# First stage of a fused linear-attention and gated-MLP kernel: work in turns that every engine keeps, with another order of norms, folds, products and sums

## The chip, the cores and the metric

One core of a Trainium2 chip runs the kernel. The metric is the device time of one execution in microseconds (us); several executions are timed, and the median is given.

## What is computed

The input `x` has 2048 rows (tokens) of 1024 numbers, all float32. Cut to what matters:

```
xn = layernorm(x)
q, k, v = split(xn @ wqkv)                # 32 heads of 32
pq, pk = q @ w_phi, k @ w_phi             # per head, 32x32
phi = concat(softmax(p), softmax(-p))     # for q and for k
o = phi_q (phi_k^T v) / (phi_q . sum(phi_k))
s = o @ wo
g = silu((sigmoid(xn @ w_gate) * (xn @ w_up)) @ w_down)
out = x + s * g
```

## The kernel before, in words

The matrix products are done by a scheme that halves both matrices in both directions and needs seven block products, with sums of blocks ahead of and behind them, in place of eight. The seven block products have names: B11, B21, T2, T3, T4, T1, B22, in this order for the projections (`order`, line 366). Each is carried out in split float32: an operand is kept as a rounded high part and a rest (`split`, line 173: a cast on ScalarE, line 175, and a difference on VectorE, line 176), and each product is three matmuls (`mm3`, line 178: lines 180, 181, 182).

Tokens go in two halves (c = 0 and 1) of 1024, in tiles of 128. For each half the stages are: projections to v, k and q (`ops`, line 372), then the gate and up products, and at the end down products, attention and output. One block product of a projection ("a group" below) is four units u, one for each tile of 128 tokens of a block, of four k steps of three matmuls 128x512: 48 matmuls. B21 is added in the same bank (PSUM) as B11, so B11's unit is copied out first (`proj_out`, line 456: lines 468 and 471 on ScalarE, 465 on VectorE).

The first stage makes what these groups need:

- `x_load` (201) loads a tile of x; `norm_steps` (205) makes statistics on VectorE (212, 213, 215), a square root on ScalarE (216), six small operations on VectorE (218 to 224) and the normalizing itself on ScalarE (227).
- `transpose` (241) does eight 128x128 transposes on TensorE (247) into two of the four banks of the ring `tps` (197). For tiles 0 to 3 the two blocks are split into operands of B11 and B21 (`operand`, 233) and also copied out (250).
- `x_sums` (252) subtracts blocks on GpSimd, in pieces of 128x256 (`Pieces`, line 79), for T1, T3, T2 and T4, and splits T2's and T3's operands at once; `x_rest` (839) splits those of B22, T1 and T4.
- v's weights are loaded in four blocks of 1 MB (`v_load`, 306), used straight by B11 and B21, summed (`v_sums`, 310: half on VectorE, line 315, half on GpSimd) for the others and stored in DRAM. `prep` (410) splits the next 128x1024 of weights into a ring of eight slots.
- The weights of k and q are folded with w_phi (`fold`, 348): for each of four k a set of four loads from `wqkT`, four times four small matmuls against a block-diagonal matrix `bd` (357), a copy (361 for k, 359 for q) and four sums on GpSimd and seven stores (`w_sums`, 283). They take their banks from the same ring `tps`.

The order before: tile 0 is traced under a high priority, the rest hangs in a deque `side`, of which `step()` runs one item after each unit of the projection (line 946). The program is scheduled ahead of time by a model that fills an engine's idle time with what is ready by its reckoning and comes earliest in the trace, so the order on each engine need not be that of the trace. `tc.issue_after(i)` puts the instructions of a block that run on the engine of i behind i in that engine's queue, without a wait for its end. SyncE (SP) issues all loads and stores in one queue.

Of the kernel before, what the change touches and what calls it, by code (L numbers as in the profile page):

```python
# [94 lines left out]
def hedgehog_glu_kernel(  # L95
# [90 lines left out]


    side = deque()

# [8 lines left out]

    last_norm = []
# [5 lines left out]
    def norm_steps(tiles, xs):  # L205
        n = len(tiles)
# [22 lines left out]
    def norm(tiles, xs):  # L229
        for _ in norm_steps(tiles, xs):  # L230
# [10 lines left out]
    def transpose(t, xt, dst):  # L241

        th, u = t // 4, t % 4
        for q in range(2):
            tp = tps.next()
            for k in range(4):
                nc.tensor.transpose(tp[:, k * P:(k + 1) * P], xt[:, (4 * q + k) * P:(4 * q + k + 1) * P], ident)
            if th == 0:
                operand(0, (B11, B21)[q], u, tp)
            nc.scalar.copy(dst[q], tp)  # L250

    def x_sums(c, u, first, second):
        (b11, b21), (b12, b22) = first, second
        t2 = b22 if c else b12
        for i, o, a, b in ((T1, b11, b12, b11), (T3, b12, b22, b12), (T2, t2, b22, b11), (T4, b21, b21, t2)):
            pool.sub(o, a, b)
            if c or i in (T2, T3):
                operand(c, i, u, o)

# [46 lines left out]
    def v_load(i):  # L306
        r, f, kh = ((39, 0, 0), (41, 0, 1), (45, 1, 0), (36, 1, 1))[i]
        nc.sync.dma_start(row4(r), v_block(f, kh))

    def v_sums():  # L310
        vec, pl = nc.vector.tensor_tensor, pool.tensor_tensor
        for f, o, a, b, op in ((vec, 3, 2, 3, "add"), (vec, 2, 0, 2, "subtract"),
                               (pl, 0, 3, 0, "subtract"), (pl, 1, 1, 0, "subtract")):
            for h in range(2):
                f(whole(VA[o] + h), whole(VA[a] + h), whole(VA[b] + h), op=getattr(ALU, op))
        for i in (T2, T3, T1, B22):
            nc.sync.dma_start(wf_d[V, i], row4(v_first[i]))

# [27 lines left out]
    o_r = Ring((36, 37, 38))  # L346

    def fold(which, k):

        bs = halves(*fblock[which].next())  # L350
        for b, (f, h) in zip(bs, ((0, 0), (0, 1), (1, 0), (1, 1))):
            r = fraw.next()
            nc.sync.dma_start(r, wqkT[which, f, k + 4 * h].rearrange("p g n -> p (g n)"))
            ps = tps.next()
            for g in range(4):
                gs = slice(g * P, (g + 1) * P)
                nc.tensor.matmul(ps[:, gs], r[:, gs], bd[:, 4 * f + g], start=True, stop=True)
            if which == Q:
                nc.scalar.copy(b.rearrange("p (a g d) -> p g a d", a=2, d=DH), ps.rearrange("p (g a d) -> p g a d", a=2, d=DH))
            else:  # L360
                nc.scalar.copy(b, ps)
        w_sums(which, k, *bs)

# [251 lines left out]
    def x_task(t):  # L615
# [18 lines left out]
        if th:  # L634
            x_sums(1, u, halves(53), halves(54))

# [176 lines left out]


    XS = (24, 25, 26, 27, 52, 53, 24, 25)
    first = [halves(i) for i in (50, 51, 54, 38)]
    b12s, b22s = Ring(halves(10)), halves(8, 9)
    xts = [x_load(0, XS[0])]
    v_load(0)
    xts += [x_load(t, XS[t]) for t in range(1, 4)]  # L820
    v_load(1)
    xts += [x_load(t, XS[t]) for t in range(4, 6)]

    def x_tiles(*tiles):
        norm(tiles, [xts[t] for t in tiles])
        for t in tiles:
            if t < 4:
                transpose(t, xts[t], first[t])
            else:
# [3 lines left out]
            if t < 2:  # L833
                xts.append(x_load(t + 6, XS[t + 6]))
            if t == 1:
                v_load(2)
                v_load(3)

    def x_rest():
        for i, name, src in ((B22, "x1", b22s), (T1, "x2", [b[0] for b in first]), (T4, "x6", [b[1] for b in first])):  # L840
            block(name, XO[i], 4, F32R)
            for u in range(4):
                operand(0, i, u, src[u])
        fraw.items = halves(43, 54)

    with tc.high_priority():
        x_tiles(0)
    with tc.issue_after(last_norm[0]):
        while prep():
            pass  # L850
    one = whole(44)[:, :P]
    nc.gpsimd.memset(one, 1.0)
    nc.scalar.copy(ones, one)
    phraw = whole(47)[:, :KT * DH].rearrange("p (g f) -> p g f", f=DH)
    nc.sync.dma_start(phraw, w_phi.rearrange("(g p) f -> p g f", p=P))
    nc.gpsimd.memset(bd, 0.0)
    for j in range(4):
        nc.gpsimd.tensor_copy(bd[j * DH:(j + 1) * DH, :, j * DH:(j + 1) * DH], phraw[j * DH:(j + 1) * DH])

    def todo(f, *a):  # L860
        side.append(lambda: f(*a))
# [12 lines left out]
    pmm = Ring(banks[:4])  # L874
    gmm = Ring(banks[:4])
    pbank, gbank = {}, {}
    ur = Ring(halves(50, 51))
# [57 lines left out]
    for n, (kind, c, what, i) in enumerate(ops):  # L935
        ws = ready[n]
        if kind == "proj":
            for u in range(4):
                if i in opening:
                    pbank[u] = pmm.next()  # L940
                xo = run(XO[i], 4)
                us = slice(u * P, (u + 1) * P)
                for k in range(4):
                    mm3(pbank[u], (xo[:, k, 0, us], xo[:, k, 1, us]), pair(ws[k]),
                        i in opening and k == 0, k == 3, skip_group_check=True)
                step()
# [281 lines left out]
```

## Time and profile before

| what | us |
|---|---|
| three runs | 2400.01, 2396.53, 2404.08 |
| median | 2400.01 |
| the profiled execution | 2394.26 |
| its span in the trace | 2392.5 |
| TensorE busy in the span | 2345.4 |

The profile is of one execution. TensorE is called PE, its weight loads PEld, VectorE DVE, ScalarE ACT, GpSimd POOL. Times in views are counted from the start of the span. The granted clock is given as a share of full speed. A busy matmul includes its tail in the pipeline, so neighbours overlap. In a view, `<-` behind a group names what it reads, and "[idle before <-releaser]" is how long the engine stood still before it and what ended that.

### The profile page before, as it was taken

The page shows a single profiled execution, that of the slowest core. Times are in us where ns is not written, and L with a number is a line of the kernel's source. Part 1 is how long each engine was busy: PE and PEld are TensorE (multiplying, and loading weights), DVE is VectorE, ACT ScalarE, POOL GpSimd, SP SyncE. Part 2 cuts the span into 40 slices and gives each one's busy share as a digit, 9 for nine tenths or more (in the row PEclk, how much of TensorE's full clock was granted, in tenths as well). Part 3 has the DMA queues.
Part 4 walks back from the last instruction along what each step waited for, and adds up shares of the span by engine and source line. Part 5 has one row for each costly group of instructions (what it writes and reads, how often), then busy time and mean ns, then how long its engine had stood idle before and what let it go on. Part 6 is the DMA issues. An engine that isn't in the chain of part 4 may idle for free.

```text
span 2392.5 us, 32528 instructions
## 1 busy us (share of the span) xinstructions
PE 2345.4 (98%) x10728; PEld 1946.9 (81%) x10728; DVE 1645.7 (69%) x2341; ACT 996.3 (42%) x1482; POOL 1206.9 (50%) x1394
## 2 busy tenths in 40 slices
PE   6999999999999999999999999999999999999998
PEld 5888888888888878887888888888888888888887
DVE  7434788777777666466767778765666786567775
ACT  6432344445454444223434343443434333345442
POOL 5630166757767532305775424244544455533766
PEclk9999999999999999999999999999999999999999
DMA  7884566788888889858998676669777877878664
GB/s 283 261 276 168 169 232 221 259 293 306 298 299 302 278 300 359 297 196 299 346 328 326 228 234 220 229 223 353 244 243 250 274 238 252 283 245 301 207 194 159
DMA packets 266426, 626.23 MB, mean 262 GB/s; under 512 B 37904, under 2 KB 66576, under 8 KB 261648
## 3 DMA queue, kind: packets, MB, share of 16 engines
q1 hardware_dynamic: 266256, 624.15, 76.3%
q8 instruction: 84, 1.38, 0.2%
q14 instruction: 86, 0.70, 0.1%
HBM read 374.47 MB, written 249.56 MB: 261 GB/s over the span
## 4 chain that ended last, share of the span: by engine, by line
PE 59%; POOL 6%; DMA 4%; issue 4%; DVE 2%; ACT 1%; SPq 0%; POOLq 0%; DVEq 0%; ACTq 0%
PE bank L180 19%; PE bank L181 19%; PE bank L182 19%; POOL fc L79 4%; POOL fb L79 1%; PE bank L558 1%; DMA fa<-w_down 1%; DMA fc<-xo_d 1%; POOL x L79 1%; DVE x L176 0%; DMA out<-fc 0%; ACT x L175 0%; DVE w L176 0%; DMA xo_d<-fc 0%; DMA fc<-f_d 0%
## 5 line engine op out<-in xcount | busy, mean ns | idle before, releaser
L181 PE MATMUL bank<-x,w 128*128 128x512 f32 x2352 | 916.3, 390 | 0.0
L180 PE MATMUL bank<-x,w 128*128 128x512 f32 x2352 | 907.0, 390 | 7.9 <-DMA w<-ws_d 4.7
L182 PE MATMUL bank<-x,w 128*128 128x512 f32 x2352 | 905.1, 389 | 0.0
L79 POOL TENSOR_TENSOR fc<-fc 128x256 f32<-128x256 f32 x496 | 420.3, 880 | 455.0 <-DMA fc<-e_d 112.3
L176 DVE TENSOR_TENSOR w<-fa,w 128x512 fp32r<-128x512 f32 (+1 forms) x444 | 406.9, 920 | 196.7 <-ACT w L175 192.6
L175 ACT CAST w<-fa 128x512 fp32r<-128x512 f32 (+1 forms) x444 | 306.8, 698 | 531.2 <-PE bank L181 318.2
L180 PEld LDWEIGHTS bank<-x,w 128*128 128x128 f32 x2352 | 442.1, 188 | 101.9 <-issue 5.1
L182 PEld LDWEIGHTS bank<-x,w 128*128 128x128 f32 x2352 | 442.1, 188 | 91.7
L181 PEld LDWEIGHTS bank<-x,w 128*128 128x128 f32 x2352 | 442.2, 188 | 90.2
L180 PE MATMUL bank<-w,x 128*128 128x512 f32 x708 | 279.2, 395 | 10.5 <-ACT fc L468 4.0
L182 PE MATMUL bank<-w,x 128*128 128x512 f32 x708 | 278.0, 393 | 3.3 <-DVE x L176 3.3
L181 PE MATMUL bank<-w,x 128*128 128x512 f32 x708 | 277.4, 392 | 0.0
L79 POOL TENSOR_TENSOR fb<-fa 128x256 f32<-128x256 f32 x112 | 100.8, 922 | 248.8 <-PE bank L182 129.6
L79 POOL TENSOR_TENSOR fb<-fb,fc 128x256 f32<-128x256 f32 x132 | 121.7, 944 | 140.1 <-DVE fc L1011 138.6
L180 PEld LDWEIGHTS bank<-w,x 128*128 128x128 f32 x708 | 133.9, 189 | 41.8 <-ACT x L175 5.5
L182 PEld LDWEIGHTS bank<-w,x 128*128 128x128 f32 x708 | 133.7, 189 | 32.9 <-DVE x L176 5.6
L181 PEld LDWEIGHTS bank<-w,x 128*128 128x128 f32 x708 | 133.8, 189 | 26.6
L79 POOL TENSOR_TENSOR fc<-fc,sa 128x256 f32<-128x256 f32 x128 | 98.5, 801 | 95.2 <-issue 86.0
L175 ACT CAST p<-fc 128x512 fp32r<-128x512 f32 x100 | 75.4, 758 | 143.8 <-DVE fc L531 61.2
L176 DVE TENSOR_TENSOR x<-fa,x 128x512 fp32r<-128x512 f32 x112 | 92.4, 825 | 49.7 <-ACT x L175 49.4
L176 DVE TENSOR_TENSOR p<-fc,p 128x512 fp32r<-128x512 f32 x100 | 96.4, 970 | 39.0 <-ACT p L175 38.9
L175 ACT CAST w<-fb 128x512 fp32r<-128x512 f32 (+1 forms) x114 | 71.0, 624 | 113.3 <-PE bank L181 85.8
(205 smaller groups left out, 2915.7 us busy)
## 6 DMA issues: line engine op xcount, KB each, us to landing
ws_d<-w SPq DMA_DIRECT2D x112, 512.0 KB, 4.3
w<-ws_d SPq DMA_DIRECT2D x112, 512.0 KB, 5.2
fa<-w_gu SPq DMA_DIRECT2D x84, 512.0 KB, 4.7
fa<-h_d SPq DMA_DIRECT2D x84, 512.0 KB, 5.2
fa<-wf_d SPq DMA_DIRECT2D x32, 1024.0 KB, 6.5
h_d<-fc SPq DMA_DIRECT2D x120, 256.0 KB, 5.2
fa<-w_down SPq DMA_DIRECT2D x80, 256.0 KB, 5.1
h_d<-fb SPq DMA_DIRECT2D x76, 256.0 KB, 4.8
```

Of the source, the lines that this page charges most:

```text
L79: self.engine.tensor_tensor(o[:, s], a[:, s], b[:, s], op=op)
L175: nc.scalar.copy(o[0], src)
L176: return nc.vector.tensor_sub(o[1], src, o[0].bitcast(F32))
L180: nc.tensor.matmul(o, a[0], b[0], start=first, stop=False, **kw)
L181: nc.tensor.matmul(o, a[0], b[1], start=False, stop=False, **kw)
L182: nc.tensor.matmul(o, a[1], b[0], start=False, stop=last, **kw)
L558: nc.tensor.matmul(kvb[g // 2][:, g % 2 * 256:g % 2 * 256 + 256], v[:, g].rearrange("p a f -> p (a f)"), ph[:, g].rearrange("p a f -> p (a ...
```

## The change

A context manager `turn()` is new. Each turn puts every instruction that it traces behind the last instruction, on the same engine, of all turns before. The first stage, with all of the first two groups (B11 and B21 of v, tokens' half 0), is a list of such turns, and the groups' loop skips these two. Within the list:

- w_phi comes in another layout (1 KB per partition) and is loaded first; tile 0, two inputs of k's first fold, tile 1, v's first block in two halves, tiles 2 and 3, the other two fold inputs, v's second block in two halves, tiles 4 and 5 and v's last blocks follow.
- Each tile's normalizing is a `tensor_scalar` on VectorE in place of an activation on ScalarE (later tiles, in `x_task`, keep ScalarE). Two of the four copies of `bd`'s diagonal go to ScalarE.
- The first fold of k is done in between: two of its four products ahead of tile 0's transposes, the others around unit 1 of B11.
- The units go B11 of tiles 0 and 1, B21 of tiles 0 and 1, B11 of tiles 2 and 3, B21 of tile 2, B21 of tile 3, with tiles 4 to 7 normalized and transposed in between.
- x's sums for T3 and T2 are made by an own function, T2 as b22 - b12 + b11 formed by an addition to T3's block; those for T4 and T1 come later (`x_late`), as does the last of v's sums. The other folds, `x_late` and `x_rest` stay in `side`, which now begins with the third group.

The diff, cut to its core:

```diff
+    turns_last = {}
+    @contextmanager
+    def turn():
+        traced = nc.cur_bb.bb.instructions
+        mark = traced[-1]
+        with ExitStack() as behind:
+            for i in list(turns_last.values()):
+                behind.enter_context(tc.issue_after(i))
+            yield
+        start = next(k for k in reversed(range(len(traced))) if traced[k] is mark) + 1
+        for i in traced[start:]:
+            turns_last[i.engine] = i
...
         for i, xt in enumerate(xs):
-            last_norm[:] = [nc.scalar.activation(xt, xt, AF.Identity, bias=b[:, i:i + 1], scale=r[:, i:i + 1]).ins]
+            if fast:
+                nc.vector.tensor_scalar(xt, xt, r[:, i:i + 1], b[:, i:i + 1], op0=ALU.mult, op1=ALU.add)
+            else:
+                nc.scalar.activation(xt, xt, AF.Identity, bias=b[:, i:i + 1], scale=r[:, i:i + 1])
...
-    def x_tiles(*tiles):
-        norm(tiles, [xts[t] for t in tiles])
-        for t in tiles:
-            if t < 4:
-                transpose(t, xts[t], first[t])
-            else:
-                b = b12s.next(), b22s[t - 4]
-                transpose(t, xts[t], b)
-                x_sums(0, t - 4, first[t - 4], b)
...
-    with tc.high_priority():
-        x_tiles(0)
-    with tc.issue_after(last_norm[0]):
-        while prep():
-            pass
...
-    todo(x_tiles, 1)
-    todo(x_tiles, 2, 3)
-    todo(x_tiles, 4, 5)
-    todo(v_sums)
-    todo(x_tiles, 6, 7)
-    for k in range(4):
-        todo(fold, K, k)
-    todo(x_rest)
-    for k in range(4):
-        todo(fold, Q, k)
+    def x_sums0(u):
+        b11, b12, b22 = first[u][0], b12s[u], b22s[u]
+        pool.sub(b12, b22, b12)
+        operand(0, T3, u, b12)
+        pool.add(b11, b12, b11)
+        operand(0, T2, u, b11)
+
+    def x_late(*us):
+        for u in us:
+            (b11, b21), b22 = first[u], b22s[u]
+            pool.sub(b21, b21, b11)
+            pool.sub(b11, b22, b11)
...
+    with turn():
+        nc.sync.dma_start(whole(47)[:, :KT * DH], w_phi)
+    for f, *a in ((x_in, 0), (fold_load, K, 0, 0), (fold_load, K, 0, 1), (x_in, 1)):
+        with turn():
+            f(*a)
+    v_load(0, 2)
+    for f, *a in ((x_in, 2), (x_in, 3), (fold_load, K, 0, 2), (fold_load, K, 0, 3)):
+        with turn():
+            f(*a)
+    v_load(1, 2)
+    for t in (4, 5):
+        with turn():
+            x_in(t)
+    v_load(2)
+    v_load(3)
+    for f, *a in (
+            (constants,), (diagonal,),
+            (norm, 0), (products_f, 0), (copies_f, 0), (norm, 0), (norm, 0), (products_f, 1),
+            (turned, 0), (prep,), (copies_f, 1), (norm, 1), (split_x, 0, 0), (prep,), (norm, 1), (norm, 1),
+            (copy_x, 0), (product, 0, 0), (x_in, 6), (turned, 1), (split_x, 1, 0), (split_x, 0, 1), (split_x, 1, 1), (copy_x, 1),
+            (products_f, 2), (norm, 2, 3), (product, 0, 1), (x_in, 7), (prep,), (out_v, 0, 0), (products_f, 3), (copies_f, 2, 3),
+            (prep,), (norm, 2, 3), (norm, 2, 3), (out_v, 0, 1), (w_sums, K, 0, *halves(4, 5)),
+            (product, 1, 0), (product, 1, 1), (turned, 2), (turned, 3),
+            (v_sum, vec, 3, 2, 3, ALU.add), (v_sum, vec, 2, 0, 2, ALU.subtract), (v_sum, pl, 0, 3, 0, ALU.subtract),
+            (split_x, 2, 0), (split_x, 3, 0), (out_v, 1, 0), (out_v, 1, 1), (norm, 4, 5),
+            (product, 0, 2), (split_x, 2, 1), (split_x, 3, 1), (copy_x, 2), (copy_x, 3), (norm, 4, 5), (norm, 4, 5),
+            (product, 0, 3), (done,), (out_v, 0, 2), (out_v, 0, 3),
+            (turned, 4), (turned, 5), (copy_x, 4), (copy_x, 5), (norm, 6, 7),
+            (product, 1, 2), (prep,), (prep,), (norm, 6, 7), (norm, 6, 7),
+            (x_sums0, 0), (turned, 6), (turned, 7), (out_v, 1, 2), (x_sums0, 1), (product, 1, 3), (done,),
+            (copy_x, 6), (copy_x, 7), (out_v, 1, 3), (x_sums0, 2), (x_sums0, 3),
+            (v_keep, T1), (v_keep, T3), (v_keep, T2)):
+        with turn():
+            f(*a)
+    folded.pop((K, 0))
+    while prep():
+        pass
+
+    def v_rest():
+        v_sum(pl, 1, 1, 0, ALU.subtract)
+        v_keep(B22)
+
+    for f, *a in ((fold, K, 1), (v_rest,), (x_late, 0, 1, 2, 3), (x_rest, T4), (fold, K, 2), (fold, K, 3),
+                  (x_rest, B22, T1), (fold, Q, 0), (fold, Q, 1), (fold, Q, 2), (fold, Q, 3)):
+        side.append(lambda f=f, a=a: f(*a))
...
         if kind == "proj":
+            if n < 2:
+                continue
             for u in range(4):
```

Here `norm` called three times for the same tiles does its three parts in turn: statistics up to the square root, the six small operations, the normalizing. `product`, `turned`, `split_x`, `copy_x`, `copies_f`, `products_f` and `out_v` do what lines 939 to 945, 247, 237, 250, 361, 357 and 456 did, for the group, tile or unit named.

## Rows read from the trace of the kernel before

**Rows 1.** the page's busy table: busy us, share, instructions.

```profile
PE 2345.4 (98%) x10728; PEld 1946.9 (81%) x10728; DVE 1645.7 (69%) x2341; ACT 996.3 (42%) x1482; POOL 1206.9 (50%) x1394
```

**Rows 2.** busy us by stretch: length, engines (x instructions), clock, DMA share, GB/s.

```profile
0.00:30.00 30.00, 15.64 (x59) 10.90 (x60) 23.25 (x56) 18.61 (x28) 8.33 (x16) 1.00 0.98 365
30.00:60.00 30.00, 26.36 (x139) 21.82 (x138) 20.20 (x30) 21.77 (x36) 24.72 (x30) 0.94 0.53 200
60.00:110.00 50.00, 46.57 (x275) 40.22 (x273) 20.55 (x24) 19.72 (x33) 41.03 (x48) 1.00 0.84 272
110.00:200.00 90.00, 89.84 (x436) 74.28 (x435) 35.84 (x44) 30.70 (x43) 22.62 (x32) 1.00 0.70 238
```

**Rows 3.** waits of PE, whole span: us in total, times, longest us.

```profile
PE bank L247 <- ACT x L227: 9.9, 3, 9.0
PE bank L180 <- DMA w<-ws_d: 4.7, 1, 4.7
```

**Rows 4.** 0 to 110 us, lines 180, 247 and 357 alone, as in rows 2.

```profile
0.00:110.00 110.00, 33.16 (x79) 15.83 (x79) 0.98 0.79 278
0.00:110.00 110.00, 8.98 (x64) 7.82 (x64) 0.98 0.79 278
0.00:110.00 110.00, 22.05 (x168) 20.96 (x168) 0.98 0.79 278
```

**Rows 5.** timeline of PE: start us, us, engine line operation.

```profile
11.27 0.79 PE L180 MATMUL bank<-w,x 128*128 128x512 f32 x1 [0.33 <-ACT x L175]
...
22.88 1.09 PE L247 MATMUL bank<-ident,x 128*128 128x128 f32 x8 [0.43 <-ACT x L227]
...
55.20 0.79 PE L182 MATMUL bank<-w,x 128*128 128x512 f32 x1 [0.84 <-DVE x L176]
...
58.35 0.42 PE L180 MATMUL bank<-w,x 128*128 128x512 f32 x1
...
101.18 0.39 PE L180 MATMUL bank<-w,x 128*128 128x512 f32 x1
101.40 0.39 PE L181 MATMUL bank<-w,x 128*128 128x512 f32 x1
```

**Rows 6.** timeline, the first fold, behind the second group.

```profile
49.10 1.05 PE L357 MATMUL bank<-fb 128*128 128x128 f32 x8
```

**Rows 7.** timeline of tile 0, tile 1's data and w_phi's.

```profile
4.47 1.28 DVE L212 BATCH_NORM_STATS2 bn<-x 128x6 f32<-128x512 f32 x2 [4.47 <-DMA x<-xk]
...
7.61 1.24 ACT L227 ACTIVATE x<-x,lnw 128x1024 f32<-128x1024 f32 x1 [1.19 <-DVE lnw L224]
...
8.53 1.29 DVE L212 BATCH_NORM_STATS2 bn<-x 128x6 f32<-128x512 f32 x2 [0.96 <-DMA x<-xk]
...
17.10 3.31 POOL L858 COPY fb<-fc 32x256 f32<-32x256 f32 x4 [13.77 <-DMA fc<-w_phi]
```

**Rows 8.** line 540: ns min/median/max, first and last start; GpSimd at the last.

```profile
L540 DVE COPY fc<-fc x2: 687/958/1228, 245.8 to 1281.9; 128x1024 f32<-128x1024 f32 x2
...
1281.49 2.20 POOL L79 TENSOR_TENSOR fb<-fb,fc 128x256 f32<-128x256 f32 x2 [5.18 <-DVE fc L1011]
```

**Rows 9.** groups by form, VectorE and ScalarE, 0 to 60 us.

```profile
L176 DVE TENSOR_TENSOR w<-fa,w 128x1024 fp32r<-128x1024 f32 x6 | 7.5, 1243 | 5.6 <-ACT w L175 5.6
L176 DVE TENSOR_TENSOR x<-bank,x 128x512 fp32r<-128x512 f32 x8 | 5.2, 674 | 0.0
L176 DVE TENSOR_TENSOR w<-fb,w 128x1024 fp32r<-128x1024 f32 x2 | 3.5, 1744 | 0.0
...
L175 ACT CAST w<-fa 128x1024 fp32r<-128x1024 f32 x6 | 6.1, 1055 | 0.0
```

**Rows 10.** tile lnw, 0 to 60 us: duration ns min/median/max, first and last start.

```profile
L223 DVE TENSOR_TENSOR lnw<-lnw x5: 106/159/655, 7.2 to 38.1; 128x2 f32<-128x2 f32 x3, 128x1 f32<-128x1 f32 x2
```

**Rows 11.** timeline of GpSimd: sums in pieces of 128x256.

```profile
68.22 2.38 POOL L79 TENSOR_TENSOR x<-x 128x256 f32<-128x256 f32 x2
...
92.16 7.61 POOL L79 TENSOR_TENSOR x<-x 128x256 f32<-128x256 f32 x8 [0.18 <-DMA wf_d<-x]
```

More of the change, by code (lines that the diff above doesn't have):

```diff
@@ L1 @@
 from collections import deque
-from contextlib import ExitStack
+from contextlib import ExitStack, contextmanager
 import concourse.bass as bass
@@ L247, in transpose, with x_sums @@
                 nc.tensor.transpose(tp[:, k * P:(k + 1) * P], xt[:, (4 * q + k) * P:(4 * q + k + 1) * P], ident)
[L248 to L252, printed above, removed]
+            out.append(tp)
+        return out
+    def x_sums(u, first, second):
         (b11, b21), (b12, b22) = first, second
-        t2 = b22 if c else b12
-        for i, o, a, b in ((T1, b11, b12, b11), (T3, b12, b22, b12), (T2, t2, b22, b11), (T4, b21, b21, t2)):
+        for i, o, a, b in ((T1, b11, b12, b11), (T3, b12, b22, b12), (T2, b22, b22, b11), (T4, b21, b21, b22)):
             pool.sub(o, a, b)
-            if c or i in (T2, T3):
-                operand(c, i, u, o)
+            operand(1, i, u, o)
     def operand_steps():
@@ L811, in attend, with product @@
         return out
+    pmm = Ring(banks[:4])
+    pbank = {}
+    def product(n, u, ks=range(4)):
+        _, c, what, i = ops[n]
+        if i in opening and 0 in ks:
+            pbank[u] = pmm.next()
+        xo = run(XO[i], 4)
+        us = slice(u * P, (u + 1) * P)
+        for k in ks:
+            mm3(pbank[u], (xo[:, k, 0, us], xo[:, k, 1, us]), pair(ready[n][k]),
+                i in opening and k == 0, k == 3, skip_group_check=True)
     XS = (24, 25, 26, 27, 52, 53, 24, 25)
     first = [halves(i) for i in (50, 51, 54, 38)]
-    b12s, b22s = Ring(halves(10)), halves(8, 9)
@@ L839, in x_rest @@
[L839 to L844, printed above, removed]
-    with tc.high_priority():
-        x_tiles(0)
-    with tc.issue_after(last_norm[0]):
-        while prep():
[L850 to L853, printed above, removed]
@@ L870, in hedgehog_glu_kernel, with x_in, turned, split_x @@
-    todo(x_rest)
-    for k in range(4):
-        todo(fold, Q, k)
-    pmm = Ring(banks[:4])
+    b12s, b22s = [halves(10)[u % 2] for u in range(4)], halves(8, 9)
+    xts, tp, norms, fps = {}, {}, {}, {}
+    def x_in(t):
+        xts[t] = x_load(t, XS[t])
+    def turned(t):
+        tp[t] = transpose(xts[t])
+    def split_x(t, q):
+        operand(0, (B11, B21)[q], t, tp[t][q])
+    def copy_x(t):
+        for q, o in enumerate(first[t] if t < 4 else (b12s[t - 4], b22s[t - 4])):
+            nc.scalar.copy(o, tp[t][q])
@@ new lines, in norm, with products_f, copies_f @@
+    def norm(*tiles):
+        if tiles not in norms:
+            norms[tiles] = norm_steps(tiles, [xts[t] for t in tiles], True)
+        next(norms[tiles], None)
+    def products_f(*ns):
+        for n in ns:
+            fps[n] = fold_products(K, 0, n)
+    def copies_f(*ns):
+        for n in ns:
+            fold_copy(K, 0, n, fps[n])
+    def x_sums0(u):
[4 more added lines that the diff above has]
+        operand(0, T2, u, b11)
@@ new lines, in x_late, with x_rest @@
+    def x_late(*us):
[3 more added lines that the diff above has]
+            pool.sub(b11, b22, b11)
+    def x_rest(*which):
+        for i, name, src in ((T4, "x6", [b[1] for b in first]), (B22, "x1", b22s), (T1, "x2", [b[0] for b in first])):
+            if i in which:
+                block(name, XO[i], 4, F32R)
+                for u in range(4):
+                    operand(0, i, u, src[u])
+        if T1 in which:
+            fraw.items = halves(43, 54)
@@ new lines, in out_v, with done, constants, diagonal @@
+    def out_v(n, u):
+        proj_out(0, V, ops[n][3], u, pbank[u])
+    def done():
+        flow["used"] += 4
+    phraw = whole(47)[:, :KT * DH].rearrange("p (g f) -> p g f", f=DH)
+    one = whole(49)[:, :P]
+    vec, pl = nc.vector.tensor_tensor, pool.tensor_tensor
+    def constants():
+        nc.gpsimd.memset(one, 1.0)
+        nc.scalar.copy(ones, one)
+        nc.gpsimd.memset(bd, 0.0)
+    def diagonal():
+        for j in range(4):
+            js = slice(j * DH, (j + 1) * DH)
+            (nc.scalar.copy if j < 2 else nc.gpsimd.tensor_copy)(bd[js, :, js], phraw[js])
@@ L937, in hedgehog_glu_kernel @@
         if kind == "proj":
+            if n < 2:
+                continue
             for u in range(4):
[L939 to L945, printed above, removed]
+                product(n, u)
                 step()
```

87 lines of the change are left out of this document (39 added, 48 removed).

## The prediction

> **What bounds the kernel now.** I read the busy table first: TensorE (PE) is busy 2345.4 us of a span of 2392.5 [rows 1], so only 47.1 us of waiting can be won anywhere. The table of stretches then says where it lies: 14.4 us before 30 us, 3.6 us from 30 to 60, 3.4 us from 60 to 110, and 0.2 us from 110 to 200 [rows 2]; the other 25.5 us lie in stages that the change does not touch. In the first 60 us VectorE is busy 43.5 us and ScalarE 40.4, and from 60 to 110 GpSimd is busy 41.0 of 50 [rows 2]. PE's longest wait is for normalized tiles, 9.9 us [rows 3]. So the first stage is a chain through VectorE and ScalarE that PE waits on, then one through GpSimd.
>
> Busy time does not show what a half clock or a pipeline's tail costs, so I count work instead. Until 110 us PE did 79 matmuls of each of the three lines of a product, 237 in all, 64 transposes and 168 fold matmuls [rows 4]. At full clock neighbours start 0.228 us apart [rows 5]; a tile's eight transposes take 1.09 us and a fold's eight 1.05 [rows 5, 6], which without a tail of 0.17 (0.39 us of one product less its 0.228) is 0.115 and 0.11 us each. That is 54.0 + 7.4 + 18.5 = 79.9 us of work in 110.0 us: **a lag of 30.1 us**, and from there to 200 us PE hardly waits. The change is worth 30.1 us less the lag of its own first stage.
>
> **What the change moves.** All products, transposes and folds stay; the order on each engine is written out. From the first tile to the last product of the second group no engine may go around a late instruction. Folds cannot fill PE's gaps before the last transposes either: they take their banks from the same ring of four, in order, behind tiles 6 and 7; before, too, the first fold ran at 49.10 us, behind all transposes [rows 6]. I follow the new order with the durations of before.
>
> *Loads.* x of tile 0 lands at 4.47 us and that of tile 1, 1.57 MB later, at 8.53 [rows 7]: 0.385 MB per us. With the folded weights' 0.13 MB put first, tile 0 comes at 4.8, the first two fold inputs at 5.5 and 6.2, tile 1 at 7.6, the first half of v's weights at 8.9, its second half at 10.3, v's last blocks at 25.3. The w_phi load moves from 17.1 us (GpSimd waited 13.8 us for it, [rows 7]) to about 3.5.
>
> *Tile 0.* From data to its scale and bias took 3.14 us (4.47 to 7.61, [rows 7]). The normalizing itself goes from ScalarE's 1.24 us [rows 7] to a VectorE operation that before does not have. Nearest is a copy of 128x1024: 0.69 us once, 1.23 the other time, at 1281.9 us, beside a running sum of GpSimd [rows 8]; those are my ends for it, the low one where GpSimd rests. Tile 0 is ready at 8.65 us, against 8.85. Two folds run ahead of its transposes on a PE at half clock (a matmul every 0.45 us at half level, [rows 5]), until 8.9; the transposes follow until 10.6.
>
> *First product.* ScalarE casts v's first half at 8.9 (1.06 us) and VectorE subtracts until 11.3 (1.23 us, both [rows 9]). In VectorE's order tile 1's statistics stand next (1.65 us with their sum), so ScalarE's root, and the cast of tile 0's transposes queued behind that root, wait until 13.2: cast until 13.8, product 0 from **13.9 us, against 11.27** [rows 5]. It ends at 18.0, about as before, because before stalled within it.
>
> *VectorE from 18.0 to tile 6.* Here the sum is longest. Three splits out of a bank at 0.67; tiles 2 and 3: four statistics at 0.64 (1.28 for two, [rows 7]), two combinations at 0.20, one sum 0.17 (3.13); two differences of weights at 1.23; six small operations, 0.16 each and 0.19 with the gap to the next, and two normalizations at 0.69 (2.52); v's four sums at 1.21, as long as a difference of that size; two splits; tiles 4 and 5 (3.13); two splits; 2.52; tiles 6 and 7 (3.13); two differences; six small ones and tile 6's normalization (1.83) [rows 9, 10]. Together 30.7 us. Into it fall five waits, read off the same order, together 6.7: tile 1's transposes and their first cast (1.4), a root of 0.20 and a weights' cast of 1.06 behind tiles 3's and 7's sums (1.4 each), the second weights' cast behind three copies (1.6), a root and a short cast behind tile 5's sum (0.9). Tile 6 is ready at 55.4, four halves of transposes (1.84) and the last product (2.74) end at **60.1 us**. Before, PE was through with the same products and transposes at 49.10 [rows 6], but four fold products (3.5 us) are now behind them too.
>
> *GpSimd beside it.* Its sums of the first fold lie at 27.7 to 33.7 us, x's sums from about 51 on. Beside a working GpSimd a weights' difference took 1.74 us instead of 1.23 [rows 9], and a small operation up to 0.66 instead of 0.16 [rows 10], of which I take 0.50 with the gap. Three differences (+1.53), one group of six small ones (+1.86), two sums (+0.66) and one normalization (+0.54) would add 4.6: **64.7 us**. Splits out of banks stay at 0.67 beside it.
>
> *The lag.* At that time PE has done 96 x 0.228 + 64 x 0.115 + 32 x 0.11 = 32.8 us of work: a lag of 27.3 us undisturbed, 31.9 disturbed. [...] From there x's operands for the next two groups come in time. I cost their later waits at nothing: ready products can stand between folds; without that cover, the 3.4 us of waiting from 60 to 110 us [rows 2], scaled by the 12 fold products still to do of the 18 that ran there, 2.3 us, come on top. Sum: 28.8 to 33.4, against 30.1: **-1.3 to +3.3 us**, up to +5.6 with the fold waits. I take the middle, +1 us. SP's queue: v's kept sums now leave behind the last copy of the second group, at about 61 us. The load that takes the place of one of them (the fifth group's weights) needs those 3 MB and its own 1 MB, 10.9 us at 0.385, and the fifth group starts past 85 us, so nothing waits there.
>
> The profiled execution took 2394.26 us, the median of three runs is 2400.01, 5.8 higher. The sum is a difference, so I put it on the median: **2401.0 us**.
>
> **Rivals.** *VectorE's waits overlap after all (faster).* The 6.7 us of waits in the chain are mine, from a strict reading of the order. If ScalarE's casts lie ahead of each of them, and GpSimd disturbs nothing, the stage ends at 53.4 and the lag is 20.6 + 1.55 = 22.2: -8 us, **2392**. For it: VectorE rests 9.8 us between 30 and 60 us [rows 2], so it is not full there, and ScalarE rests 8.2. Against it: the new order puts ScalarE's root between two casts for each pair of tiles, and that root needs VectorE's latest sum. Without the clock's loss too it is -9.5.
>
> *GpSimd's late sums (slower).* x's sums for the fifth and sixth group now stand behind the second fold's eight pieces and v's eight. x's first sums end at about 68 us; the last operand of the fifth group is 30 pieces later, and PE wants it at 64.7 + 1.55 + 21.9 + 3.5 + 8.2 = 99.8, with 1.3 us of split before. It decides from 1.02 us a piece. Pieces took 0.95 us (7.61 for eight) and 1.19 in other rows [rows 11]. If the planner also puts the third fold's eight pieces ahead, at 0.95 the operand is 5.6 us late; with the fold waits, +1 + 5.6 + 2.3 = +9: **2409**.
>
> [...] In the rows, the copy that shared its time with GpSimd was 0.54 us longer, and a price of 1.23 for each of eight moves the disturbed end from 64.7 to 68.3: +3.3 + 3.6 = +6.9, **2407**. [...]
>
> *The order doesn't hold, or later stages are planned anew.* The remainder is scheduled again around other times; a wait like the largest single one (4.7 us for a reloaded weight, [rows 3]) may come or go: 2396 or 2406.
>
> **How the numbers follow.** Forecast 0.50, first rival 0.23, GpSimd 0.14, port 0.08, planned anew 0.05. About 0.3% (7.2 us) is what a measurement of this kernel can tell from none. The faster rival lies at that bound and beyond (0.20 of its 0.23), and I give the forecast's own spread 0.04; slower takes GpSimd's 0.13, half of the port's and 0.03 of the spread. That makes 0.24 faster, 0.56 the same, 0.20 slower. The range reaches from -12 (the first rival without the clock's loss, -9.5, and half a wait of 4.7 us less later) to +12 (GpSimd's rival with the disturbed end, +9 + 2.3): 2388 to 2412.
>
> **What would show it.** Right: the first product of v near 13.9 us, the end of the second group between 60 and 65 us, PE's longest waits after 20 us on the normalizations of tiles 4 to 7, normalizations at 0.69 and 1.23 us, and hardly a wait from 65 to 110. Wrong: an end of that group near 53 us (the waits overlapped), or PE waiting at 85 to 110 us for a split behind a GpSimd sum. Wrong altogether would be a lag at 110 us under 22 or over 38.

## The result, and the profile after

The changed kernel took 2410.02 us (median of six runs, 2405.09 to 2412.44), the kernel before beside it 2398.61 (six runs, 2395.51 to 2404.08): a ratio of 1.0048 with a 95% interval of 1.0034 to 1.0062. It is slower, by more than the 0.3% within which I had put it, and inside the range given. The profiled execution took 2410.48 us, its span is 2408.7.

The stretches of the changed kernel, in the columns of [rows 2]:

```profile
0.00:30.00 30.00, 17.01 (x79) 14.06 (x79) 16.29 (x37) 15.26 (x26) 2.53 (x10) 0.88 0.95 353
30.00:60.00 30.00, 19.82 (x86) 15.98 (x85) 27.26 (x47) 11.35 (x22) 26.64 (x29) 0.84 0.30 115
60.00:110.00 50.00, 48.25 (x263) 40.94 (x264) 30.29 (x30) 22.80 (x37) 40.35 (x44) 0.93 0.73 255
110.00:200.00 90.00, 83.21 (x414) 70.88 (x413) 32.54 (x38) 29.47 (x43) 31.87 (x40) 0.96 0.77 259
```

From 30 to 60 us PE is busy 6.5 us less than before, and the granted clock is on record below full in all four stretches, where before it was so in one. (In the kernel before, too, PE began at about half speed, which the 1.00 of its first row doesn't show: until 17.3 us its matmuls took 0.63 us and started 0.43 apart, later 0.40 and 0.23, and tile 0's eight transposes took 1.94 us, a later tile's 1.09.) The last row is the surprise: PE is busy 83.2 us of 90 where before had 89.8.

The three largest of PE's waits up to 170 us (us in total, times, longest):

```profile
PE bank L368 <- DMA fb<-wqkT: 12.9, 2, 6.8
PE bank L180 <- ACT x L175: 9.8, 3, 5.0
PE bank L258 <- DVE fc L241: 5.0, 1, 5.0
```

PE's timeline at the places where they fall:

```profile
14.93 0.80 PE L180 MATMUL bank<-w,x 128*128 128x512 f32 x1 [4.47 <-ACT x L175]
...
48.78 3.65 PE L258 MATMUL bank<-ident,fc 128*128 128x128 f32 x16 [5.02 <-DVE fc L241]
...
60.63 0.79 PE L180 MATMUL bank<-w,x 128*128 128x512 f32 x1 [4.98 <-ACT x L175]
...
61.91 3.68 PE L258 MATMUL bank<-ident,x 128*128 128x128 f32 x16
...
125.52 2.05 PE L368 MATMUL bank<-fb 128*128 128x128 f32 x8 [6.79 <-DMA fb<-wqkT]
...
128.69 0.47 PE L180 MATMUL bank<-w,x 128*128 128x512 f32 x1
```

The first product comes at 14.93 us. The transposes of tiles 4 and 5 wait 5.0 us for their normalizing and then take 3.65 us for the sixteen of two tiles, where one tile's eight took 1.09 [rows 5]: half clock behind the wait (granted 0.50 from 48.78 to 53.3 us). The next two rows and the last two show the same again (3.68 us for sixteen, at a granted 0.50; a fold's eight 2.05, against 1.05 in [rows 6], at 0.50 until 128.4 us). The wait of 5.0 us at 60.63 is put down to a cast for the third group, two of whose matmuls stand ahead of the transposes of tiles 6 and 7; these had to wait until tile 6 was normalized, at 61.9, in any case.

The wait of 6.8 us ends at 125.5, among the side work, where the change had altered little but the order. What it waited for, the load of a fold's input, was issued by SP right behind a store of k's fourth fold (SP's timeline):

```profile
121.30 0.32 SPq L293 DMA_DIRECT2D wf_d<-x  x1
121.71 0.38 SPq L362 DMA_DIRECT2D fb<-wqkT  x1
```

That store had to wait for GpSimd's sums, which ended at 121.3 (below).

VectorE's timeline in the changed kernel, small operations and normalizations ahead of and beside GpSimd's work:

```profile
31.33 0.16 DVE L236 TENSOR_TENSOR lnw<-lnw 128x2 f32<-128x2 f32 x1
...
31.73 1.54 DVE L241 TENSOR_SCALAR x<-x,lnw 128x1024 f32<-128x1024 f32 x2
...
46.09 0.64 DVE L236 TENSOR_TENSOR lnw<-lnw 128x2 f32<-128x2 f32 x1
...
47.45 2.31 DVE L241 TENSOR_SCALAR fc<-fc,lnw 128x1024 f32<-128x1024 f32 x2
...
60.66 2.32 DVE L241 TENSOR_SCALAR x<-x,lnw 128x1024 f32<-128x1024 f32 x2
```

GpSimd's timeline (k's first fold, v's sums in two rows, x's first sums, k's fourth fold):

```profile
33.36 9.93 POOL L79 TENSOR_TENSOR x<-x 128x256 f32<-128x256 f32 x8 [29.49 <-DMA wf_d<-x]
43.25 5.96 POOL L79 TENSOR_TENSOR fa<-p,fa 128x256 f32<-128x256 f32 x8
49.18 7.04 POOL L79 TENSOR_TENSOR fa<-fa 128x256 f32<-128x256 f32 x8
56.18 2.38 POOL L79 TENSOR_TENSOR x<-x 128x256 f32<-128x256 f32 x2
...
113.74 7.53 POOL L79 TENSOR_TENSOR x<-x 128x256 f32<-128x256 f32 x8 [6.57 <-DMA wf_d<-x]
```

Alone, a small operation takes 0.16 us and two normalizations 1.54 (0.81 for one); from 33.4 us on GpSimd works without a gap, and they take 0.64 and 2.31.

As in the prediction I count the lag of PE's work: the time less 0.228 us for each matmul of a product (18 starts from 100.03 to 103.90 us in the kernel before lie that far apart), 0.115 for a transpose and 0.11 for a fold matmul that has run by then (counts by line, as in [rows 4]; for the products three times line 180's count, since some records of single matmuls are missing). Here is the lag of every kernel of this study, with the start of the casts of B22's x operands (the first row of line 175 that writes x from x, four at once), which turned out to matter. Each label stands again at its experiment below; every lag is of one profiled execution.

| kernel | 50 us | 70 | 110 | 130 | B22's casts, us | ratio |
|---|---|---|---|---|---|---|
| before | 19.9 | 25.9 | 30.1 | 31.7 | 108.1 | 1 |
| changed | 25.7 | 35.2 | 37.4 | 45.6 | 124.2 | 1.0048 |
| no_turns | 16.8 | 26.9 | 35.3 | 35.7 | 110.9 | 1.0015 |
| act_norm | 26.4 | 36.5 | 37.4 | 47.9 | 125.8 | 1.0109 |
| folds_apart | 25.7 | 34.2 | 38.2 | 41.5 | 101.5 | 1.0045 |
| fold_late | 27.4 | 36.9 | 37.1 | 49.4 | 134.3 | 1.0101 |
| stores_act | 25.3 | 33.4 | 37.4 | 42.2 | 121.0 | 1.0057 |
| vector_free | 21.8 | 32.9 | 32.6 | 42.9 | 120.1 | 1.0039 |
| vector_apart | 21.8 | 31.6 | 31.2 | 33.1 | 98.0 | 1.0018 |
| no_turns_apart | 18.0 | 28.2 | 34.2 | 34.9 | 92.8 | 1.0017 |
| pool_turns | 18.6 | 20.6 | 30.4 | 39.8 | 115.4 | 1.0033 |
| pool_turns_stores | 19.1 | 27.4 | 32.2 | 44.5 | 122.0 | 1.0061 |
| pool_turns_apart | 19.1 | 22.8 | 35.0 | 34.7 | 102.6 | 0.9985 |
| pool_turns_apart_vec | 18.7 | 20.6 | 27.0 | 28.5 | 99.6 | 0.9981 |

At 170 us the changed kernel's lag is 46.2 and that of before 31.9: 14.3 of the 16.2 us between the two profiled executions lie ahead of 170 us. 7.3 of them had come by 110 us, the other 7.0 later, nearly all of it by 130. After that the stages differ little; from 170 to 500 us PE is busy throughout in both.

### The profile page after: what moved, and what is told of

Its sections match the earlier page's. It is cut to its first block, busy times and chain, and to the rows that moved or that the text cites. A ratio compares the mean times of both kernels' runs of the same rounds, so it can differ in the third digit from the quotient of the medians.

```text
span 2408.7 us, 32520 instructions
## 1 busy us (share of the span) xinstructions
PE 2350.0 (98%) x10728; PEld 1952.4 (81%) x10728; DVE 1660.1 (69%) x2349; ACT 988.6 (41%) x1476; POOL 1212.0 (50%) x1392
## 4 chain that ended last, share of the span: by engine, by line
PE 52%; POOL 7%; DMA 6%; issue 5%; DVE 3%; ACT 1%; SPq 0%; POOLq 0%; DVEq 0%; ACTq 0%
PE bank L180 17%; PE bank L181 17%; PE bank L182 17%; POOL fc L79 5%; DMA fa<-w_down 1%; POOL fb L79 1%; PE bank L581 1%; POOL x L79 1%; DVE x L176 1%; DMA wo_d<-p 1%; DVE w L176 1%; DMA fc<-wo 1%; DMA fc<-w_down 1%; DMA g_d<-x 0%; DMA fc<-g_d 0%
## 5 line engine op out<-in xcount | busy, mean ns | idle before, releaser
L79 POOL TENSOR_TENSOR fc<-fc 128x256 f32<-128x256 f32 x502 | 425.9, 880 | 452.2 <-DMA fc<-e_d 115.1
```

The lines of the kernel that those rows point to most:

```text
L79: self.engine.tensor_tensor(o[:, s], a[:, s], b[:, s], op=op)
```

## The experiments

Ratios are to the kernel before on the same chip. The diffs are against the changed kernel.

### First: which part of the change costs

*Without the order of the turns* (`no_turns`). The turns trace the same list but bind nothing.

```diff
-            for i in list(turns_last.values()):
-                behind.enter_context(tc.issue_after(i))
```

> The changed kernel with the same work in the same trace order, but turn() adds no order: each engine's order is the scheduler's again. Theory (two causes: the VectorE chain of the first 68 us, and a second wait at 118 to 128 us for slots that the third and fourth fold of k hold): the first part shrinks, by 3 to 7 us of the 11 lost, the second can stay, so 2403 to 2407 us. Rival (the strict order alone costs it): back to 2399 us or below.

2398.41 us (12 runs, 2392.44 to 2404.93), ratio 1.0015 (1.0003 to 1.0027). The order itself costs some 8 us of the 11, more than the theory's 3 to 7; the rival's time held. Free to go around a late instruction, the list is good: lag 16.8 us at 50, three less than before. Then it loses 8 us by 60. PE's timeline of this kernel:

```profile
59.85 0.80 PE L180 MATMUL bank<-w,x 128*128 128x512 f32 x1 [8.23 <-ACT x L175]
```

And GpSimd's:

```profile
47.99 9.35 POOL L79 TENSOR_TENSOR x<-x 128x256 f32<-128x256 f32 x8
57.30 3.22 POOL L79 TENSOR_TENSOR fc<-x,fc 128x256 f32<-128x256 f32 x4
```

The x sums of the third group are those of fc<-x,fc, and PE waits 8.2 us for what hangs on them. Ahead of them GpSimd does eight pieces x<-x in 9.35 us: four of k's first fold (its other four ran before 45 us) and four of x's sums for T3, on which T2's are built. So about half of that row is the fold's.

*Normalizing on ScalarE again, within the turns* (`act_norm`).

```diff
-            norms[tiles] = norm_steps(tiles, [xts[t] for t in tiles], True)
+            norms[tiles] = norm_steps(tiles, [xts[t] for t in tiles], False)
```

> The changed kernel with the normalizing back on ScalarE (1.24 us each), the turns unchanged. Theory (VectorE's chain sets the end of the first stage): eight operations of 0.8 to 1.15 us leave the chain, of which ScalarE's give back a part; the second group ends 2 to 5 us earlier and the time falls by as much. Rival (ScalarE between VectorE's steps sets it): 2 to 5 us slower.

2420.0 us (2409.65 to 2424.87), ratio 1.0109 (1.0094 to 1.0124): the move to VectorE is worth some 0.6% within these turns. The theory failed, and the rival had the direction but not the size. The profile is of the run of 2409.65 us and shows a lag of 49.0 at 170 us against 46.2, so only part of this difference is seen in it.

*K's third and fourth fold in other slots, 52 and 53* (`folds_apart`, line 289):

```diff
-    fblock = {K: Ring(((4, 5), (6, 7))), Q: ...
+    fblock = {K: Ring(((4, 5), (6, 7), (52, 53), (52, 53))), Q: ...
```

> The changed kernel with the third and fourth fold of k in other slots (52, 53), so that the seventh group's operand no longer waits for their stores. Theory: the wait at 118 to 128 us (6.8 us and a half clock behind it) goes, 5 to 8 us faster, 2402 to 2405. Rival (PE's order is fixed behind the fold whose load came late, or the lag is all of the first 68 us): no change.

2404.49 us (2402.77 to 2413.04), ratio 1.0045 (1.0031 to 1.006). One row of ScalarE's timeline shows what the slots do, first in the changed kernel:

```profile
124.18 2.18 ACT L175 CAST x<-x 128x512 fp32r<-128x512 f32 x4 [4.83 <-DMA wf_d<-x]
```

And in this one:

```profile
101.54 2.18 ACT L175 CAST x<-x 128x512 fp32r<-128x512 f32 x4 [1.12 <-DMA wf_d<-x]
```

These are the casts of the x operands for B22, v's seventh and last group. They write into slots 4 to 7, which k's folds hold until their sums are made on GpSimd and stored. The group that PE wants first is the sixth, T1. Its operands go into slots 8 to 11, where the blocks lie from which B22's are cast, so T1's casts stand right behind B22's. In the changed kernel:

```profile
127.36 1.66 ACT L175 CAST x<-fc 128x512 fp32r<-128x512 f32 x3 [1.00 <-DVE x L176]
```

With the slots apart B22's casts come 22.6 us earlier, PE's wait of 6.8 us is gone (its longest between 85 and 170 us is 1.0), the rise of the lag between 110 and 130 us falls from 8.2 to 3.3, and the lag at 170 us from 46.2 to 41.5. The ratio hardly moves: inconclusive by itself. (PE's wait from 118.7 us on is put down to a fold's load, since a fold's product stood next in its queue; no product of T1 could have run before its casts at 127.36 either, and the first came at 128.69.)

*The first fold left out of the turns* (`fold_late`), as the first item of `side`:

```diff
-    for f, *a in ((x_in, 0), (fold_load, K, 0, 0), (fold_load, K, 0, 1), (x_in, 1)):
+    for f, *a in ((x_in, 0), (x_in, 1)):
...
-    for f, *a in ((fold, K, 1), (v_rest,), (x_late, 0, 1, 2, 3), (x_rest, T4), (fold, K, 2), (fold, K, 3),
+    for f, *a in ((fold, K, 0), (fold, K, 1), (v_rest,), (x_late, 0, 1, 2, 3), (x_rest, T4), (fold, K, 2), (fold, K, 3),
```

(its products, copies and sums are taken out of the list likewise)

> The changed kernel with the first fold of k taken out of the turns and put at the head of the side work. Theory: GpSimd's sums at 33 to 43 us no longer disturb VectorE, and the second group ends 3 to 6 us earlier (PE also does 3.5 us less before it), but four folds instead of three must pass before the seventh group, so the second wait grows: the time stays within 4 us of the changed kernel. Rival (the early fold is what costs): 7 to 11 us faster, as before.

2417.65 us (2416.21 to 2426.33), ratio 1.0101 (1.0084 to 1.0117). Both theory (within 4 us) and rival (faster) failed: the lag at 70 us is no smaller (36.9 against 35.2), and the early fold is a gain within the turns. Without it four folds stand ahead of B22's casts in place of three; these start at 134.3 us, and the lag reaches 55.3.

### Second: the wait at 118 to 126 us, and whose order costs

*The unchanged blocks of each fold stored from ScalarE* (`stores_act`, line 292), so that they don't queue on SP behind stores that wait for GpSimd:

```diff
-        def keep(i, b):
-            nc.sync.dma_start(wf_d[which, i, :, k], b)
+        def keep(i, b, q=nc.sync):
+            q.dma_start(wf_d[which, i, :, k], b)
 
-        for i, b in ((B11, a11), (B21, a12), (T4, a22)):
-            keep(i, b)
+        for i, b in ((T4, a22), (B21, a12), (B11, a11)):
+            keep(i, b, nc.scalar)
```

> The changed kernel, but the three blocks of each fold that are stored as they are (B11, B21, T4) are issued from ScalarE right behind the fold's copies, in place of SP's queue; T4 goes first. Theory (the second wait, at 118 to 128 us, is made by SP's queue: k's stores and the next loads stand in it behind stores that wait for GpSimd): GpSimd's sums of k's folds, which waited 5.6 and 6.6 us for their own stores, run without those waits, the wait of 6.8 us at 118 to 126 us goes, the lag of PE's work at 170 us falls from 46 to about 38, and the ratio to the kernel before from 1.0048 to about 1.001 to 1.002. Rival (the second wait is made by the number of folds still to do, not by the queue): GpSimd's sums start earlier, but the lag at 170 us stays above 43 and the ratio at 1.004 or more.

2406.48 us (2404.56 to 2410.61), ratio 1.0057 (1.0045 to 1.0069). GpSimd's waits ahead of the third and fourth fold shrank (5.56 to 1.60, 6.57 to 4.96 us), but B22's casts still came at 121.0 and the lag at 170 us was 42.8. The rival held, but for 0.2 us of lag. This does not clear SP's queue: the edit moved three of seven stores. GpSimd's sums of the fourth fold ended at 112.8 in place of 121.3, but the last of its four other stores left SP only at 116.79, behind a store of v's result, and the next fold's load behind that at 117.26. A kernel with these stores out of SP's queue as well was not run.

*VectorE out of the turns* (`vector_free`).

```diff
-            for i in list(turns_last.values()):
+            for i in [i for i in turns_last.values() if i.engine != nc.vector.engine]:
```

> The changed kernel with turns that bind every engine but VectorE. Theory (VectorE's written order is what the first 68 us lose): VectorE takes the next tiles' statistics early, the last transposes run near 50 us in place of 62 and the lag of PE's work at 50 us falls from 25.7 to under 20; the time falls by 4 to 8 us, ratio about 1.001 to 1.003. Rival (PE's or ScalarE's order holds the stage): the lag at 50 us stays at 24 or more, and the ratio at 1.004 to 1.006.

2403.16 us (2398.59 to 2407.12), ratio 1.0039 (1.0027 to 1.0052). A lag of 21.8 at 50 us and a ratio of 1.0039 lie between what theory and rival had, and the ratio is not clear of the changed kernel's 1.0048. At 110 the lag is 32.6, five less than with all turns. By 130 most of it is gone: 42.9 against 45.6. What the first stage gained, the wait for B22's casts took (they start at 120.1 us).

*Only GpSimd bound, x's sums ahead of the first fold's* (`pool_turns`). The condition above reads `== nc.gpsimd.engine`, and `(w_sums, K, 0, ...)` stands behind `(x_sums0, 3)` in the list.

> Turns that bind GpSimd alone, and the sums of k's first fold moved behind x's last sums in the list. Without any turns the lag was 16.8 us at 50 us, then rose to 24.8 by 60 because the first fold's sums ran on GpSimd ahead of x's. Theory: with x's sums first the lag at 60 us stays near 17 to 20, and the time is 4 to 7 us below that of the kernel without turns: ratio 0.9985 to 1.0. Rival (x's sums are late even without the fold's, since v's sums and the pieces before take GpSimd's time): the lag at 60 us is 23 or more, ratio about 1.0015 as without turns.

2400.51 us (seven runs: five from 2398.48 to 2401.34, two at 2407), ratio 1.0033 (1.0022 to 1.0044). The theory's first half held (lag 20.8 at 60 us, in place of 24.8), its time did not: from 100 to 120 us the lag rises by 15, and B22's casts come at 115.4. The profile is of the run of 2407.32 us. Two things are changed at once here, who is bound and where the fold's sums stand; they were not tried apart.

*The same with the stores from ScalarE* (`pool_turns_stores`).

> Both edits: GpSimd alone bound, first fold's sums behind x's, and the folds' three unchanged blocks stored from ScalarE. Theory: it has neither the wait at 50 to 60 us nor, if SP's queue makes it, the one at 90 to 100 us: lag at 130 us 24 to 29 (31.7 in the kernel before), ratio 0.996 to 0.999, faster than both kernels. Rival (each wait that is taken away comes back at the next fold): lag at 130 us of 31 or more, ratio 1.0 or above.

2407.01 us (2403.97 to 2413.23), ratio 1.0061 (1.0048 to 1.0074). The rival's signs held (lag 44.5 at 130 us): worse than without the edit.

### Third: both causes at once

*VectorE free, and the slots apart* (`vector_apart`, the two edits above together).

> The changed kernel, VectorE not bound by the turns, and k's third and fourth fold in slots 52 and 53. Each edit alone brought little (ratio 1.0039 and 1.0045, from 1.0048). Theory now: there are two causes in a row. What the first one costs is given back at the last group of v (B22), since its x operands go into slots 4 to 7, which k's folds hold until GpSimd has done their sums; so each edit alone is masked by the other cause. Both together then give more than the sum of the two: no wait at 110 to 128 us, lag of PE's work at 170 us about 33 to 36 in place of 46 (alone 43.5 and 41.5), ratio about 1.000 to 1.002. Rival (the causes add up independently): lag about 39, ratio 1.0035.

2396.48 us (12 runs, 2393.98 to 2401.44), ratio 1.0018 (1.0008 to 1.0027). From 1.0048 each edit alone took 0.0009 and 0.0003, both together 0.0030. The lag at 130 us is 33.1, no more than 1.9 above its 31.2 at 110, and the casts no longer wait for a store (ScalarE's timeline):

```profile
98.03 2.18 ACT L175 CAST x<-x 128x512 fp32r<-128x512 f32 x4 [2.31 <-POOL fc L79]
```

The lags show two causes in a row, each hiding the other: at 170 us the edits alone take 4.7 and 2.7 us, both together 13.0 (33.2 is left). The rival's 39 us and 1.0035 failed. The ratios alone would not show it, since a plain sum of the two edits, 1.0036, has an interval of about 0.0024 to either side.

*No order, slots apart* (`no_turns_apart`).

> The changed kernel with no order from the turns, and k's third and fourth fold in slots 52 and 53. Without turns the lag was 16.8 us at 50, 24.8 at 60 (first fold's sums on GpSimd ahead of x's) and rose from 27.5 to 35.3 between 90 and 110. Theory (that second rise is B22's x operands behind the slots of k's folds): it goes; lag at 130 us 28 to 30, ratio about 0.998 to 1.0, against 1.0015. Rival (the second rise is the fold loads' place in SP's queue): lag at 130 stays at 34 or more.

2396.75 us (2393.13 to 2401.29), ratio 1.0017 (1.0007 to 1.0026): as without the edit. B22's casts ran at 92.8 us, and still the lag rose from 28.2 at 90 to 34.2 at 110, in waits for fold loads and for ScalarE's fold copies. In the free order that second rise is not B22's. The rival's sign held (34.9 at 130); that the loads' place in SP's queue makes the rise was not tested.

*GpSimd alone bound, slots apart* (`pool_turns_apart`)*; then also the sums of k's third and fourth fold on VectorE* (`pool_turns_apart_vec`; in `w_sums`, for `which == K and k > 1`, four `nc.vector.tensor_tensor` in place of `pool.add` and `pool.sub`).

> Turns that bind GpSimd alone, first fold's sums behind x's, and k's third and fourth fold in slots 52 and 53. Bound alone, the lag was 20.6 us at 70 but rose from 23.6 to 39.8 between 100 and 130, where B22's splits waited for the slots until 115 us. Theory: that rise goes, lag at 130 us 23 to 27, ratio 0.995 to 0.998: faster than both kernels. Rival (the gain of the first 60 us is given back in another way, by fold loads that come late or by GpSimd, which is full from 39 to 108 us): lag at 130 above 30, ratio 0.999 or more.

> As the kernel before it in this list, and the four sums of k's third and fourth fold on VectorE in place of GpSimd (four operations of 128x1024... here 128x512 each, in place of eight pieces of about 0.95 us). Theory: with the slots apart nothing of PE waits for those sums any more, so it is the same within 0.1% as that kernel. Rival (GpSimd's load still sets the stage's end): 2 to 5 us faster, the fold loads behind its stores come earlier, and PE's waits for fold loads between 100 and 130 us fall.

2390.28 us (2385.98 to 2396.12) and 2390.41 us (2383.91 to 2394.57), twelve runs each beside 34 of the kernel before at 2393.65: ratios 0.9985 (0.9974 to 0.9996) and 0.9981 (0.9968 to 0.9994). Both beat both kernels, the one before by 0.15 and 0.19%. That is less than the theory's 0.2 to 0.5%, and the lags at 130 us, 34.7 (with a stall, see below) and 28.5, are above its 23 to 27. By the ratios, the edit on slots took 0.5% from the kernel that binds GpSimd alone; the move of sums added nothing, as the theory had it. The second one's stretch from 60 to 130 us shows PE at 64.7 us and full clock, where the changed kernel had 61.5 at 0.90 (columns as in [rows 2]):

```profile
60.00:130.00 70.00, 64.68 (x369) 54.83 (x368) 39.68 (x48) 26.61 (x44) 44.56 (x52) 1.00 0.83 277
```

The changed kernel's:

```profile
60.00:130.00 70.00, 61.45 (x330) 52.61 (x331) 39.62 (x43) 30.79 (x50) 47.88 (x52) 0.90 0.77 266
```

The first one's profile is of the run of 2396.12 us, and has a stall of its own (last section). The kernel before with its slots apart was not run; without an order from the turns the edit brought nothing (1.0017 against 1.0015).

## Where the prediction was right and where it was wrong

The time came out 9 us above the forecast, and 11.4 above the kernel before beside it, where the forecast had 1. It lies in the range, but by luck: the upper end, 2412, was worked out from x's sums coming late on GpSimd for the fifth group, and there PE hardly waited (the lag was 37.4 us at 90 and at 110). Another wait, one group later, filled the range. By the prediction's steps:

- *First product 13.9 us*: 14.93. Tile 0 was late too (data at 5.34 in place of 4.8, normalizing 0.81 us and not 0.69), but VectorE was through with it at 9.3 and then stood 2.0 us for the cast of v's first half. That cast waited for its load until 10.23, where the sum had 8.9:

```profile
10.23 1.04 ACT L175 CAST w<-fa 128x1024 fp32r<-128x1024 f32 x1 [1.46 <-DMA fa<-wv]
```

- *VectorE from 18 us to tile 6*: nearly right. Five waits were read off the order, together 6.7 us; VectorE's five largest in this stretch are 2.06, 1.26, 1.18, 0.81 and 1.27, together 6.6. GpSimd's disturbance was put at 4.6 us and was some 6.6 by the rows named here, since the first fold's sums started at 33.4 and not 27.7 (they waited for their stores) and GpSimd then worked through: the five small operations took 3.2 to 3.3 us in two of the groups in place of 0.95 (I had counted one group), two pairs of normalizations 2.31 in place of 1.54 (I had counted one operation), and two differences of weights 2.89 in place of 2.46. Tile 6 was ready at 61.9, where the disturbed sum had 60.0.
- *The second group's end, 60.1 or 64.7 us*: about 69. From tile 6's readiness to there I had 4.6 us at full clock; it was 7, of which the first 5 at half clock (granted 0.50 from 61.91 to 66.67 us).
- *The clock's loss, 1.55 us*: mis-sized. It was an estimate from one stretch of the kernel before, seven matmuls in 3.15 us from 55.20 to 58.35 [rows 5] at a granted clock of 0.50, where 0.228 apart they would take 1.60; that the changed kernel would lose just as much, no row showed. Up to 110 us PE is busy 85.1 us for 72.6 of work, before 88.6 for 79.9. What is over, from half clock and from pipeline tails, is 12.5 against 8.7, so 3.8 us more, and 3.5 us more is idle. That is the 7.3 us of lag at 110, of which I had -1.3 to +3.3, or up to 5.6 with the fold waits.
- *"From there to 200 us PE hardly waits"*: **the step that failed.** It was read from the kernel before and used for both. In the changed kernel the next 20 us lose 6.6 us more than before, nearly as much as all of the first 110. K's second, third and fourth fold start their sums on GpSimd at 88.4, 99.6 and 113.7 us, each behind a wait for a store, and the fourth ends at 121.3 (in the kernel before, GpSimd was through with k's folds at 102.9); B22's operands need their slots, and T1's stand behind B22's. I had looked at who is late behind GpSimd, but only for x's sums, and priced the slots of the folds at nothing. That this wait hangs on the slots is shown by the two kernels with VectorE free: with the folds apart, the rise between 110 and 130 us falls from 10.3 to 1.9 us (with VectorE bound, from 8.2 to 3.3). What SP's queue adds to it, where the next loads stand behind the folds' stores, is not separated.
- *The signs*: hardly a wait from 65 to 110 us came true (the lag was 35.2 at 70 and 37.4 at 110), and one of PE's long waits was on a normalizing (5.0 us); the first product and the group's end did not.

*The rivals.* The waits of VectorE's chain did not overlap within the turns; without the turns they did (16.8 us at 50), and even that kernel was not faster than before. So the gain of the list was real at 50 us, but the stages behind it did not keep it. Late sums on GpSimd came to count in the end, but those of k's folds and not x's, and one group later than I had placed them. As for the rival at 2407 us (0.08 of the chances), a normalizing alone took 0.81 us and beside GpSimd 1.16 to 1.21: that is the longer time which the rival reckons with, for four of eight, 1.6 us in all and not the 3.6 that it put on top (its own 0.54 us for each of the seven not yet counted would be 3.8). What makes a normalizing longer beside GpSimd, no row shows. With ScalarE in its place the kernel was still slower (1.0109 against 1.0048), so the longer normalizings did not decide.

What stays open: how the rest of the order's cost divides between PE, ScalarE and SP (at 90 us the lag was 37.4 with all turns, 32.5 with VectorE free and 27.5 with none), what makes the waits for fold loads from 90 to 110 us in the free order, and how much of the wait at 118.7 us is SP's queue.

## What to carry to other kernels

An order written out for every engine can turn each late instruction into a wait for all that stands behind it (1.0048 here, against 1.0015 without the order); bind the one engine whose choice was wrong (here GpSimd, which took a fold's sums ahead of sums that PE needed) and leave the others free. That alone was no gain here (1.0033, against 1.0015 without any order); it became one when the slots were moved too (0.9985). When work is moved earlier or later, follow its buffers to the next reader as well as its engines: a gain at 60 us is worth nothing if the group at 120 us waits for slots that the moved work still holds. And where two causes stand in a row, taking away one may show almost nothing, so try them together before dropping either.

## What the runs showed of the hardware

Five of the six small operations on VectorE, which touch two numbers for each of 128 partitions, went from 0.16 to 0.65 us while GpSimd worked (0.49 to 0.66), four times as long, where two normalizations of 128x1024 took half as long again (2.31 us for 1.54) and two differences of weights a sixth longer (2.89 us for 2.46). Those five in a row took 3.3 us, more than two normalizations beside GpSimd (2.31). Not everything got longer: the sixth, a reciprocal, kept 0.15 us, four statistics 2.46, and four of v's sums 1.22 us each, as long as such a difference alone (1.23). The reciprocal beside GpSimd, and the operation behind it:

```profile
43.93 0.15 DVE L231 RECIPROCAL lnw<-lnw 128x2 f32<-128x2 f32 x1
44.12 0.56 DVE L233 TENSOR_TENSOR lnw<-lnw 128x2 f32<-128x2 f32 x1
```

Behind each of PE's four waits of 4.5 to 6.8 us between 10 and 130 us it ran at half clock for 3 to 6 us (granted 0.50 from 14.93 to 18.93, from 48.78 to 53.3, from 60.63 to 66.9 and from 125.52 to 128.4 us), and once behind a wait of 2.15 us (0.50 from 29.6 to 32.9). Up to 110 us the busy time over the work, in which this lies with the tails, grew by 3.8 us over the kernel before, about as much as the idle time (3.5).

Once, in the profile of the kernel with GpSimd alone bound and the slots apart, one VectorE operation took 13.59 us in place of the usual 0.7 to 1.25. It ended at 94.5 us, 0.6 us after GpSimd, busy without a gap from 73.65 to 93.9 us, came to rest. VectorE's timeline:

```profile
80.89 13.59 DVE L176 TENSOR_TENSOR x<-p,x 128x512 fp32r<-128x512 f32 x1 [3.29 <-ACT x L175]
```

PE's:

```profile
95.13 0.80 PE L180 MATMUL bank<-w,x 128*128 128x512 f32 x1 [9.15 <-DVE fc L488]
```

GpSimd's first and last row of that run of work:

```profile
73.65 3.77 POOL L79 TENSOR_TENSOR x<-x 128x256 f32<-128x256 f32 x4
...
91.14 2.78 POOL L79 TENSOR_TENSOR fc<-fc 128x256 f32<-128x256 f32 x4
```

PE waited 9.2 us behind it. No run shows why it lasted so long beside pieces of GpSimd of 0.7 us each. It is rare: in none of the other profiles does a single operation of VectorE last over 1.9 us in the first 200 us (the longest 1.82), though GpSimd worked without a gap in several (in the changed kernel from 33.4 to 73 us). What sets it off was not tried, and that GpSimd caused it is read from the times alone.
